# A transformer block's forward and backward on one core: the short fifth matmuls of dh in pairs of row halves, some transposes of the last head on TensorE with W_o's loads on ACT's queue, and W_q^T loaded at other places

## The chip, the core and the metric

The kernel runs on one core of a Trainium2 chip. A core has five engines with an instruction stream each: TensorE (PE, matrix multiplications into PSUM; its weight loads are listed as PEld), VectorE (DVE), ScalarE (ACT), GpSimd (POOL) and SyncE (SP), which here only issues DMA transfers. ACT and POOL issue transfers too. An engine works through its stream in order; semaphores make one engine wait for another, or for a transfer. The metric is the device time of one execution in microseconds (us); lower is better.

## The reference

The program takes one sequence of S = 2048 rows of D = 576 through a block with two branches, and returns the output and the gradients of the eight inputs (x, the K and V caches, and five weight matrices):

```python
def _A_ref(x, k_cache, v_cache, wq, wo):
    q = (x @ wq).reshape(B, Sq, H, Dh).transpose(0, 2, 1, 3)      # H 32, Dh 128
    scores = einsum("bhqd,bhkd->bhqk", q, k_cache) * (Dh ** -0.5)
    p = softmax(scores)
    o = einsum("bhqk,bhkd->bhqd", p, v_cache)
    return o.transpose(0, 2, 1, 3).reshape(B, Sq, H * Dh) @ wo

def _B_ref(x, w_gate, w_up, w_down):                              # F 4608
    g, u = einsum("bsd,df->bsf", x, w_gate), einsum("bsd,df->bsf", x, w_up)
    return einsum("bsf,fd->bsd", sigmoid(g) * u, w_down)

xn = layernorm(x)
out = x + _A_ref(xn, ...) * silu(_B_ref(xn, ...))
# and the vjp of out with grad_out, for x, k_cache, v_cache, wq, wo, w_gate, w_up, w_down
```

All matrices are bf16. Two gradients matter for what follows. With dO the gradient at the output of the second branch's last product, dh = dO @ w_down^T (2048 x 4608), du and dg are dh times two stored factors (`a_d` and `b_d`), and dw_up = xn^T @ du, dw_gate = xn^T @ dg, dw_down = h^T @ dO. The gradient at xn sums du @ w_up^T + dg @ w_gate^T + dq @ w_q^T.

## The kernel before, in words

Everything is tiled in P = 128 rows or columns; NT = 16 is the number of row tiles of S, DT = 5 the number of tiles of D. 576 is four tiles of 128 and one of KL = 64 columns; DL = 4 is the number of the short one. The stages run one after the other on TensorE:

- a1 (0 to 313 us): layernorm, gate and up projections. Full rows are multiplied at L295. The contraction over the 64 columns left over is done at L303 by pairs of matmuls on 64 of TensorE's 128 rows each, one for gate on the upper and one for up on the lower half. The stored factors a and b, and h, go to DRAM.
- a2 (to about 485): the product with w_down and what hangs on it.
- attention (to about 3655): 32 heads, one after the other but interlocked. Each head is laid on 64 positions of a programme written by hand: `at(pos, fn, ...)` enters a step at a position, `anchor` enters the steps that set the beat, and the list is then run in order of position. The order of the instructions on PE, DVE and ACT is that of the programme (`MAN`); SP's and POOL's streams are ordered by the tile framework's scheduler. A head makes P (the softmax numerators) and dS row tile by row tile, two tiles to a pair. Each pair is turned by a DMA transpose on SP (`trans_P`, `trans_dS`, issued at L603) into PT or dST, from four shared buffers (`wpt`), and PE's row products (L620, `acc<-Vn,PT` and `acc<-Kn,dST`) read these. L644 makes the column products from P and dS themselves. At the end of the last head five loads bring W_o, the heads' rows of it laid into two tiles no longer needed, by SP's queue (`load_wo`, L460).
- c1, the dO pass (to about 3807): for each row tile st, oT (the heads' outputs turned, by a DMA transpose on SP at L843, five buffers), times W_o at L872, 64 matmuls a tile; VectorE then forms the output row tile and doB = dO of the row tile, POOL loads three inputs two tiles ahead (`load_grp`, L849) and stores the output (L883). doB is turned into doBT by five TensorE transposes (L818) and two copies (`transpose_doB`). The fifth tile of doBT holds the 64 columns left over in its rows 64 to 127, and zeros above, which a memset puts there. w_down^T is loaded in three thirds of F columns (`wdT_h[0..2]`, L857, five transposes each on SP), the first third within this pass after row tiles 7, 8, 10, 11 and 12, and the others in b1.
- b1 (to about 4390): 18 blocks fb of 256 columns of F. In each: dh (L925, 16 row tiles x 5 matmuls into PSUM tiles of two row tiles; ACT copies each out at L929 as dhc, DVE multiplies it with the two factors at L930 and L931 to du_blk and dg_blk), dwd (`make_dwd`, L943, two halves, each of 16 row tiles times a 512-wide and a 64-wide matmul), the two products dwu and dwg (L967, accw, 64 matmuls each, in four groups of 16 row tiles), and their left-over 64 columns (L975, accl). The order of the engines' streams here is the scheduler's save for SP, whose order is written out.
- c2 (to about 4643): dw_q.
- c4 (to the end): the gradient at x, in eight blocks sbi of 256 rows, each in passes pi: three of du (cf), three of dg (cf), two of dq (cq) of 48 matmuls or more at L1101, into one set of PSUM accumulators a block. The first two blocks do their du and dg passes first, then their dq passes. Each pass starts with a DMA transpose on SP (L1088). W_q^T is loaded in four groups of eight heads, five DMA transposes each (`load_wqT`, `load_T_rows` at L92), after passes (0,3), (0,5), (1,1), (1,3) as (sbi, pi).

`turn` is a small job that later stages carry along: one DMA transpose of a stored gradient of K or V (L157), and the 512 KB store of the turn before (L160). There are 46 of them, spread over b1, c2 and c4; `turn(tkp, False)` only flushes the last store.

Of the kernel before, what the change touches and what calls it, by code (L numbers as in the profile page):

```python
# [95 lines left out]
def kernel(  # L96
# [80 lines left out]
    def kfull(i, kd):  # L177
        return P if KPAD else kd
# [243 lines left out]
    with tc.tile_pool(name="ld2", bufs=2) as ld2, tc.tile_pool(name="ld1q", bufs=1) as ld1q, \  # L422
# [19 lines left out]
        def at(pos, fn, *args):  # L442
            prog.append((pos, len(prog), fn, args))
# [13 lines left out]
        def load_wo(h0, h1):  # L457
            t_, o = (xnT, 0) if h0 < WX else (dsT, WX)
            dst = t_[:].rearrange("p i s -> p (i s)")[:, (h0 - o) * D:(h1 - o) * D].rearrange("p (h d) -> p h d", d=D)
            nc.sync.dma_start(dst, A_wo[h0 * P:h1 * P, :].rearrange("(h p) d -> p h d", p=P))  # L460

# [151 lines left out]
        class Box:  # L613
            pass

        def row_mm(bx, hs, T, rhs, qt, kt, sink):
            j = qt % GQ
            if j == 0 and kt == 0:
                bx.acc = ps_row.tile([P, GQ, P], f32, name="acc")
            nc.tensor.matmul(bx.acc[:, j, :], lhsT=T[qt][:, kt, :], rhs=getattr(hs, rhs)[:, kt, :],  # L620
                             start=(kt == 0), stop=(kt == NT - 1))
            if j == GQ - 1 and kt == NT - 1:
                sink(bx.acc)
# [185 lines left out]
    if True:  # L809
        pc2 = tc.alloc_tile_pool(name="pc2", bufs=1, reuse_waits="tile")  # L810
        doB = pc2.tile([P, NT, D], bf, name="doB")
        doBT = pc2.tile([P, DT, S], bf, name="doBT")
        nc.vector.memset(doBT[:P - KL, DL, :], 0.0)

        def transpose_doB(pool, st_):
            pt = pool.tile([P, 8, P], bf, name="pt", tag="tr")
            for j in range(DT):
                nc.tensor.transpose(pt[:, j, :], doB[:, st_, dlo[j]:dlo[j] + P], ident[:])  # L818
            cols = slice(st_ * P, (st_ + 1) * P)
            alt.copy(doBT[:, :DL, cols], pt[:, :DL, :])  # L820
# [8 lines left out]
        with tc.tile_pool(name="c1b", bufs=1, side="right", reuse_waits="tile") as blk, \  # L829
# [26 lines left out]
            def load_wdT(i, k=0):  # L856
                nc.sync.dma_start_transpose(wdT_h[k][:, i, :], B_w_down[k * FH:(k + 1) * FH, dlo[i]:dlo[i] + P])  # L857

            for st in range(NT):
# [30 lines left out]
        with tc.tile_pool(name="b1o", bufs=2, reuse_waits="tile") as outp, tc.tile_pool(name="b1k", bufs=2, reuse_waits="tile") as tkp, tc.tile_pool(name="b1t", bufs=3, reuse_waits="tile") as tmpp, \  # L890
                tc.tile_pool(name="b1r", bufs=2, reuse_waits="tile") as dblk, \
                tc.tile_pool(name="b1l", bufs=1, reuse_waits="tile") as ldp, \
                tc.tile_pool(name="b1ps", bufs=2, space=PSUM, reuse_waits="tile") as ps, \
                tc.tile_pool(name="b1pa", bufs=2, space=PSUM, reuse_waits="tile") as psa, \
                tc.tile_pool(name="b1pw", bufs=2, space=PSUM, reuse_waits="tile") as psw, \
# [16 lines left out]
            for fb in range(F // FB):  # L912
# [4 lines left out]
                dg_blk = dblk.tile([P, NT, FB], bf, name="dg_blk")  # L917
                def make_dh():
                    for st in range(NT):
                        srows = slice(st * P, (st + 1) * P)  # L920
                        if st % 2 == 0:
                            dh = ps.tile([P, 2, FB], f32, name="dh")
                        for i, (d0, kd) in enumerate(dts):
                            kk = kfull(i, kd)
                            nc.tensor.matmul(dh[:, st % 2, :], lhsT=doBT[:kk, i, srows], rhs=wdT_h[fb * FB // FH][:kk, i, fh], start=(i == 0), stop=(i == DT - 1))  # L925
                        if st % 2 == 1:
                            s2 = slice(st - 1, st + 1)
                            dhc = tmpp.tile([P, 2, FB], bf, name="dhc")
                            nc.scalar.copy(dhc[:], dh[:])  # L929
                            nc.vector.tensor_tensor(du_blk[:, s2, :], dhc[:], a_blk[:, s2, :], op=ALU.mult)  # L930
                            nc.vector.tensor_tensor(dg_blk[:, s2, :], dhc[:], b_blk[:, s2, :], op=ALU.mult)  # L931
                    nc.gpsimd.dma_start(du_d[:, fcols].rearrange("(t p) f -> p t f", p=P), du_blk[:])
                    nc.gpsimd.dma_start(dg_d[:, fcols].rearrange("(t p) f -> p t f", p=P), dg_blk[:])

# [15 lines left out]
                if fb == 0:  # L950
                    make_dwd(0)
                    make_dh()
                    make_dwd(1)
                else:
                    make_dh()
# [34 lines left out]
        with tc.tile_pool(name="c2b", bufs=1, reuse_waits="tile") as blk, tc.tile_pool(name="c2s", bufs=2, reuse_waits="tile") as sb, \  # L990
# [26 lines left out]
            for hg in range(NHG):  # L1017
# [43 lines left out]
        with tc.tile_pool(name="c4c", bufs=1, reuse_waits="tile") as chp, tc.tile_pool(name="c4s", bufs=2, reuse_waits="tile") as sb, \  # L1061
# [16 lines left out]
            NPF = 2 * (FT // FC)  # L1078
            accs_ = {}

            def do_pass(sbi, pi):
# [4 lines left out]
                scol = slice(sbi * SB2, (sbi + 1) * SB2)  # L1086
                ch = chp.tile([P, KC, SB2], bf, name=f"cq{pi % 2}" if nm == "cq" else f"cf{pi % 3}")
                nc.sync.dma_start_transpose(ch[:], src_d[scol, k0 * P:(k0 + KC) * P])  # L1088
# [83 lines left out]
```

## Time and profile before

| | us |
|---|---|
| median of three runs | 5063.81 |
| the three runs | 5054.67, 5063.81, 5084.64 |
| the profiled execution | 5069.4 |
| its span | 5067.4 |
| TensorE busy in it | 4914.0 |

The profile lists one execution. Times of rows are microseconds from the span's start. A group row of a view by line reads: line, engine, operation, what it writes and reads, tile size, shape and count, then busy time in us and mean ns of one, and after the last bar the idle time of the engine before it and what ended that. A row of a timeline reads: start, length, engine and line, with the idle time before it in brackets. A row of the waits reads: total us, times, the longest. The granted clock is the TensorE clock that the throttle allowed, as a share of full speed; ends of matmuls are modelled, so starts are the surer numbers. A DMA issue on a queue is shown as a row of that queue (SPq), and a row can gather several issues.

### The profile page before, as it was taken

The numbers are of one execution on the slowest core, as the hardware profiler recorded it, in microseconds if no ns is written. First come the engines' busy times: TensorE is split into PE (matmuls) and PEld (weight loads), VectorE is DVE, ScalarE is ACT, GpSimd is POOL, SyncE is SP. The second block draws the span as 40 slices with busy tenths as digits, with TensorE's granted clock in tenths as the row PEclk, the third lists the DMA queues.
The fourth block names the chain that finished last, engine by engine and source line by source line (L and its number), as shares of the span: only waits on it lengthen the run. The fifth ranks groups of instructions, "written<-read, shape, count | busy, mean of one in ns | idle before, by whom it ended". The sixth has DMA issues, their size and how long they took to land.

```text
span 5067.4 us, 107190 instructions
## 1 busy us (share of the span) xinstructions
PE 4914.0 (97%) x45178; PEld 3188.2 (63%) x45968; DVE 3098.3 (61%) x4853; ACT 2390.4 (47%) x3035; POOL 1504.2 (30%) x2197
## 2 busy tenths in 40 slices
PE   9998999999999999999999999999889999999999
PEld 3344777777766666666666666666547778755454
DVE  6555878887887888888788888888533222110101
ACT  5533656665666666566566666656302222100000
POOL 4322333333333333333333333332322323211000
PEclk9999999999999999999999999999999999999999
DMA  7875999999999999999999999999999988899996
GB/s 255 271 219 140 204 201 207 202 209 208 209 205 208 209 201 207 208 203 207 209 209 212 205 208 210 204 202 213 222 182 273 232 225 218 253 267 235 199 211 140
DMA packets 2865204, 1077.14 MB, mean 213 GB/s; under 512 B 2672336, under 2 KB 2795216, under 8 KB 2864720
## 3 DMA queue, kind: packets, MB, share of 16 engines
q1 hardware_dynamic: 2779456, 784.45, 86.6%
q0 software_dynamic: 85264, 285.79, 19.7%
q8 instruction: 359, 5.88, 0.5%
q14 instruction: 125, 1.02, 0.1%
HBM read 172.54 MB, written 225.12 MB: 78 GB/s over the span
## 4 chain that ended last, share of the span: by engine, by line
PE 84%; DVE 5%; issue 4%; DMA 3%; POOL 3%; SPq 0%; ACT 0%; DVEq 0%; POOLq 0%; ACTq 0%
PE acc L620 16%; PE acckv L644 9%; PE acc L1101 7%; PE sp L556 7%; PE dp L589 6%; PE accw L967 5%; PE acckv L641 5%; PE accp L513 4%; PE dh L925 3%; PE acc L392 3%; PE accd L943 3%; PE g_ps L295 2%; PE acc L1025 2%; PE u_ps L295 2%; PE acct L520 2%
## 5 line engine op out<-in xcount | busy, mean ns | idle before, releaser
L568 ACT ACTIVATE Pq<-sneg,nm 128x2048 bf16<-128x2048 bf16 x512 | 1025.9, 2004 | 212.0 <-DVE sneg L558 169.3
L592 DVE SCALAR_TENSOR_TENSOR dSq<-dp,delta,Pq 128x1024 bf16<-128x1024 f32 x608 | 770.8, 1281 | 390.8 <-PE dp L589 384.4
L620 PE MATMUL acc<-Kn,dST 128*128 128x128 bf16 x8192 | 955.2, 219 | 22.5 <-DMA dST<-dSq 6.4
L620 PE MATMUL acc<-Vn,PT 128*128 128x128 bf16 x8192 | 957.9, 219 | 15.9 <-DMA PT<-Pq 6.5
L620 PEld LDWEIGHTS <-dST 128*128 128x128 bf16 x8192 | 670.9, 98 | 363.9 <-DMA dST<-dSq 10.7
L620 PEld LDWEIGHTS <-PT 128*128 128x128 bf16 x8192 | 665.3, 98 | 329.8 <-DMA PT<-Pq 7.6
L558 DVE TENSOR_SCALAR_CACHE_REDUCE sneg<-sp,nm 128x1024 bf16<-128x1024 f32 x512 | 656.7, 1283 | 132.8 <-PE sp L556 101.1
L595 ACT ACTIVATE t<-dp,negdelta 128x1024 bf16<-128x1024 f32 x416 | 463.5, 1114 | 510.3 <-PE dp L589 419.8
L558 DVE TENSOR_SCALAR_CACHE_REDUCE sneg<-sp 128x1024 bf16<-128x1024 f32 x512 | 624.7, 1220 | 92.9 <-PE sp L556 45.7
L589 PE MATMUL dp<-VT,dOT 128*128 128x512 bf16 x1943 | 587.1, 379 | 26.4 <-DVE dSq L592 26.2
L556 PE MATMUL sp<-KT,QT 128*128 128x512 bf16 x1922 | 583.2, 380 | 7.3 <-DVE sneg L558 6.5
L644 PE MATMUL acckv<-Pq,dOn 128*128 128x512 bf16 x1312 | 487.5, 380 | 5.8 <-POOL dOn L576 5.8
L644 PE MATMUL acckv<-dSq,Qn 128*128 128x512 bf16 x1355 | 490.2, 380 | 1.2
L599 DVE TENSOR_TENSOR dSq<-t,Pq 128x1024 bf16<-128x1024 bf16 x416 | 304.5, 732 | 0.0
L576 POOL TENSOR_TENSOR dOn<-dOn,rinv_all 128x256 bf16<-128x256 bf16 x256 | 157.2, 614 | 390.2 <-DVE rinv_all L572 322.7
L967 PEld LDWEIGHTS <-xn_all 128*128 128x128 bf16 x2304 | 224.2, 98 | 27.8
L1117 DVE SCALAR_TENSOR_TENSOR junk<-dxn,xn_all 128x576 f32<-128x576 f32 x16 | 12.1, 758 | 370.9 <-ACT dxn L1112 370.9
L1101 PEld LDWEIGHTS <-cf 128*128 128x128 bf16 x2304 | 145.8, 98 | 145.6 <-DMA cf<-du_d 5.6
L513 PE MATMUL accp<-xnT,wq_h 128*128 128x512 bf16 x609 | 227.8, 384 | 4.4 <-ACT KT L40 1.1
L641 PE MATMUL acckv<-dOn,Pq 128*128 128x128 bf16 x2304 | 217.3, 219 | 2.8 <-POOL dOn L576 1.4
L674 POOL TENSOR_TENSOR prod<-ou,dOn 128x512 f32<-128x512 bf16 x128 | 154.8, 1209 | 207.5 <-ACT ou L40 206.7
L641 PE MATMUL acckv<-Qn,dSq 128*128 128x128 bf16 x2304 | 213.9, 219 | 1.4
(188 smaller groups left out, 7461.6 us busy)
## 6 DMA issues: line engine op xcount, KB each, us to landing
out_dram<-turn SPq DMA_DIRECT2D x46, 512.0 KB, 4.7
h_d<-h_row POOLq DMA_DIRECT2D x48, 384.0 KB, 2.9
a_d<-a_row POOLq DMA_DIRECT2D x48, 384.0 KB, 3.4
b_d<-b_row POOLq DMA_DIRECT2D x48, 384.0 KB, 4.5
a_blk<-a_d SPq DMA_DIRECT2D x18, 1024.0 KB, 6.0
b_blk<-b_d SPq DMA_DIRECT2D x18, 1024.0 KB, 21.7
du_d<-du_blk POOLq DMA_DIRECT2D x18, 1024.0 KB, 8.7
dg_d<-dg_blk POOLq DMA_DIRECT2D x18, 1024.0 KB, 11.7
```

Source lines behind the costliest of these rows:

```text
L513: nc.tensor.matmul(acc[:], lhsT=w[:, i, :], rhs=(srcT if i < DL else xnT)[:, i, cs], start=(i == 0), stop=(i == DL))
L556: nc.tensor.matmul(sp[:, c * CH:(c + 1) * CH], lhsT=hs.QT[:, qs], rhs=hs.KT[:, hf * HW_ + c * CH: hf * HW_ + (c + 1) * CH], start=True, st ...
L558: nc.vector.tensor_scalar(sneg[:, hf * HW_:(hf + 1) * HW_], sp[:], -SCALE, None if hf == 0 else nm[:, hf - 1:hf], op0=ALU.mult, op1=ALU.mi ...
L568: nc.scalar.activation(Pq, sneg[:], AF.Exp, bias=nm[:, hf:hf + 1], scale=-1.0, accum_out=hs.rs_all[:, qt:qt + 1])
L589: nc.tensor.matmul(dp[:, c * CH:(c + 1) * CH], lhsT=hs.dOT[:, qs], rhs=hs.VT[:, hf * HW_ + c * CH: hf * HW_ + (c + 1) * CH], start=True, s ...
L592: nc.vector.scalar_tensor_tensor(dSq[:, hsl], dp[:], hs.delta[:, qt:qt + 1], Pq[:, hsl], op0=ALU.subtract, op1=ALU.mult)
L595: nc.scalar.activation(t[:], dp[:], AF.Identity, bias=hs.negdelta[:, qt:qt + 1], scale=1.0)
L620: nc.tensor.matmul(bx.acc[:, j, :], lhsT=T[qt][:, kt, :], rhs=getattr(hs, rhs)[:, kt, :], start=(kt == 0), stop=(kt == NT - 1))
L641: nc.tensor.matmul(bx.acc[i][:, j * P:(j + 1) * P], lhsT=slabs[qt][:, k0 + j * P:k0 + (j + 1) * P], rhs=w, start=(qt == 0 and j == 0), sto ...
L644: nc.tensor.matmul(bx.acc[i][:], lhsT=w, rhs=slabs[qt][:, k0:k0 + CH], start=(qt == 0), stop=(qt == NT - 1))
L967: nc.tensor.matmul(acc[:kd, :FB], lhsT=xn_all[:, st, d0:d0 + kd], rhs=blk_[:, st, :], start=(st == 0), stop=(st == NT - 1))
L1101: nc.tensor.matmul(accs[sl][j][:, :nn], lhsT=ch[:, kk, sl * P:(sl + 1) * P], rhs=w_[:, n0:n0 + nn], start=(pi == 0 and kk == 0), stop=(las ...
```

## The change

The diff has five pieces.

1. dh in two halves. The 16 row tiles of a block are made as `make_dh(0)`, `make_dwd(0)`, `make_dh(1)`, `make_dwd(1)`. Each half first does the four full matmuls of its eight row tiles into four PSUM tiles, and then their fifth matmuls as four pairs: one of a pair on rows 0 to 63, the other, of a row tile two further on, on rows 64 to 127. For that both halves of the fifth tile of doBT and of wdT hold the same 64 columns: `transpose_doB` gets a third copy, `load_wdT` a DMA on POOL from the tile's lower to its upper half after the fifth transpose, and the memset goes. The PSUM pool of dh has four buffers in place of two, that of dwd one in place of two.
2. In the last head W_o is loaded in 15 pieces on ACT's queue, at positions 1.3 + 4k of the head, in place of five on SP's from position 50.
3. In the last head three pairs, P (14,15), dS (6,7) and dS (14,15), are turned on TensorE: 96 transposes into PSUM (`pe_pair`) with a copy out for each 8 or 16.
4. W_q^T's third and fourth groups are loaded after passes (1,3) and (1,5); the dq passes of the first two blocks alternate, (0,6), (1,6), (0,7), (1,7), and cq's buffers are counted through.
5. One turn less in c2 and one less in the second block of c4, so that as many places are left as there are turns, and the last flush stands behind the last block's stores.

```diff
-            nc.sync.dma_start(dst, A_wo[h0 * P:h1 * P, :].rearrange("(h p) d -> p h d", p=P))
+            nc.scalar.dma_start(dst, A_wo[h0 * P:h1 * P, :].rearrange("(h p) d -> p h d", p=P))
...
+        def pe_pair(T, pairs, qt, name, n, pool, tag, i, eng):
+            if i == 0:
+                t_ = wpt.tile([P, 2 * NT, P], bf, name=name, tag="PT")
+                for j in range(2):
+                    T[qt + j] = t_[:, j * NT:(j + 1) * NT, :]
+            pt = pool.tile([P, n, P], bf, name="ptr", tag=tag)
+            for m in range(n):
+                j, kt = divmod(i * n + m, NT)
+                nc.tensor.transpose(pt[:, m, :], pairs[qt][:, j, kt * P:(kt + 1) * P], ident[:])
+            j, kt = divmod(i * n, NT)
+            alt.copy(T[qt + j][:, kt:kt + n, :], pt[:], eng=eng)
...
-        WO_AT = 50.0
+        WO_AT = [(i, min(i + 2, 14)) for i in range(0, 14, 2)] + [(14, WX)] + [(i, min(i + 2, WX + WD)) for i in range(WX, WX + WD, 2)]
+        P_PE = {NT - 2: (35.5, 37.5, 39.5, 41.5)}
+        DS_PE = {6: (48.5, 50.5, 52.5, 54.5), NT - 2: (65.5, 67.0)}
...
-                    at(p1 + PT_AT, trans_P, hs, qt - 1)
-                    at(p2 + DST_AT, trans_dS, hs, qt - 1)
+                    if h == H - 1 and qt - 1 in P_PE:
+                        for i, p_ in enumerate(P_PE[qt - 1]):
+                            at(b + p_, pe_pair, hs.PT, hs.Pp, qt - 1, "PT", 8, ps_tr, "tr", i, "s")
+                    else:
+                        at(p1 + PT_AT, trans_P, hs, qt - 1)
...
-        for k, (h0, h1) in enumerate(((0, 8), (8, 16), (16, WX), (WX, WX + 7), (WX + 7, WX + WD))):
-            if h0 < H - 1:
-                at(bl + WO_AT + 3 * k, load_wo, h0, min(h1, H - 1))
+        for k, (h0, h1) in enumerate(WO_AT):
+            at(bl + 1.3 + 4 * k, load_wo, h0, h1)
...
-        nc.vector.memset(doBT[:P - KL, DL, :], 0.0)
...
             alt.copy(doBT[P - KL:, DL, cols], pt[P - KL:, DL, :])
+            alt.copy(doBT[:KL, DL, cols], pt[P - KL:, DL, :])
...
                 nc.sync.dma_start_transpose(wdT_h[k][:, i, :], B_w_down[k * FH:(k + 1) * FH, dlo[i]:dlo[i] + P])
+                if i == DL:
+                    nc.gpsimd.dma_start(wdT_h[k][:KL, DL, :], wdT_h[k][P - KL:, DL, :])
...
+                def make_dh(half):
+                    w_ = wdT_h[fb * FB // FH]
+                    sts = range(half * NT // 2, (half + 1) * NT // 2)
+                    dhs = [ps.tile([P, 2, FB], f32, name="dh") for _ in sts[::2]]
+                    for k, st in enumerate(sts):
+                        for i in range(DL):
+                            nc.tensor.matmul(dhs[k // 2][:, k % 2, :], lhsT=doBT[:, i, st * P:(st + 1) * P], rhs=w_[:, i, fh],
+                                             start=(i == 0 and k % 2 == 0), stop=False)
+                    for k in (0, 1, 4, 5):
+                        for j in range(2):
+                            rs = slice(j * KL, (j + 1) * KL)
+                            st = sts[k + 2 * j]
+                            nc.tensor.matmul(dhs[k // 2 + j][:, k % 2, :], lhsT=doBT[rs, DL, st * P:(st + 1) * P], rhs=w_[rs, DL, fh],
+                                             start=False, stop=(k % 2 == 1))
...
                 else:
-                    make_dh()
                     for fl in range(FB // P):
+                        make_dh(fl)
                         make_dwd(fl)
...
-                if hg < NHG - 1:
+                if hg < NHG - 2:
                     turn(tkp)
...
-                ch = chp.tile([P, KC, SB2], bf, name=f"cq{pi % 2}" if nm == "cq" else f"cf{pi % 3}")
+                ch = chp.tile([P, KC, SB2], bf, name=f"cq{next(ncq) % 2}" if nm == "cq" else f"cf{pi % 3}")
...
-                if sbi == 0 and pi in (3, 5):
-                    load_wqT((3, 5).index(pi))
-                elif sbi == 1 and pi in (1, 3):
-                    load_wqT(2 + (1, 3).index(pi))
-                elif sbi and sbi < NSB - 1 and (pi % 4 == 1 or (pi == 3 and sbi > 1)):
+                if (sbi, pi) in WQ_AT:
+                    load_wqT(WQ_AT.index((sbi, pi)))
+                elif 1 < sbi < NSB - 1 and pi in (1, 3, 5):
                     turn(tkp)
...
-            order_ = [(sbi, pi) for sbi in range(2) for pi in range(NPF)] + [(sbi, pi) for sbi in range(2) for pi in range(NPF, len(passes))]
+            order_ = [(sbi, pi) for sbi in range(2) for pi in range(NPF)] + [(sbi, pi) for pi in range(NPF, len(passes)) for sbi in range(2)]
```

More of the change, by code (lines that the diff above doesn't have):

```diff
@@ L1 @@
+import itertools
 from contextlib import ExitStack
@@ L782 @@
                 if qt % 2:
-                    at(p1 + PT_AT, trans_P, hs, qt - 1)
-                    at(p2 + DST_AT, trans_dS, hs, qt - 1)
+                    if h == H - 1 and qt - 1 in P_PE:
[3 more added lines that the diff above has]
+                        at(p1 + PT_AT, trans_P, hs, qt - 1)
+                    if h == H - 1 and qt - 1 in DS_PE:
+                        for i, p_ in enumerate(DS_PE[qt - 1]):
+                            if len(DS_PE[qt - 1]) == 4:
+                                at(b + p_, pe_pair, hs.dST, hs.dSp, qt - 1, "dST", 8, ps_tr, "tr", i, "s")
+                            else:
+                                at(b + p_, pe_pair, hs.dST, hs.dSp, qt - 1, "dST", NT, ps_big, "big", i, "sv"[i])
+                    else:
+                        at(p2 + DST_AT, trans_dS, hs, qt - 1)
                 if qt not in STT2:
@@ L917 @@
                 dg_blk = dblk.tile([P, NT, FB], bf, name="dg_blk")
[L918 to L933, printed above, removed]
@@ new lines, in make_dh @@
+                def make_dh(half):
[12 more added lines that the diff above has]
+                                             start=False, stop=(k % 2 == 1))
+                    for k, dh in enumerate(dhs):
+                        s2 = slice(sts[2 * k], sts[2 * k] + 2)
+                        dhc = tmpp.tile([P, 2, FB], bf, name="dhc")
+                        nc.scalar.copy(dhc[:], dh[:])
+                        nc.vector.tensor_tensor(du_blk[:, s2, :], dhc[:], a_blk[:, s2, :], op=ALU.mult)
+                        nc.vector.tensor_tensor(dg_blk[:, s2, :], dhc[:], b_blk[:, s2, :], op=ALU.mult)
+                    if half == 1:
+                        nc.gpsimd.dma_start(du_d[:, fcols].rearrange("(t p) f -> p t f", p=P), du_blk[:])
+                        nc.gpsimd.dma_start(dg_d[:, fcols].rearrange("(t p) f -> p t f", p=P), dg_blk[:])
@@ L1079 @@
             accs_ = {}
+            ncq = itertools.count()
+            WQ_AT = [(0, 3), (0, 5), (1, 3), (1, 5)]
             def do_pass(sbi, pi):
```

7 lines of the change are left out of this document (4 added, 3 removed).

## The prediction

> **What bounds the kernel now.** I read the page's head first, then the split of the span by stage, then what TensorE waited for in each stage the diff touches.
>
> ```profile
> span 5067.4 us, 107190 instructions
> PE 4914.0 (97%) x45178; PEld 3188.2 (63%) x45968; DVE 3098.3 (61%) x4853; ACT 2390.4 (47%) x3035; POOL 1504.2 (30%) x2197
> ...
> 3524.00:3653.00 129.00, 107.22 (x937) 68.53 (x953) 83.44 (x120) 59.80 (x65) 34.19 (x46) 0.93 1.14 220
> 3653.00:3807.00 154.00, 140.00 (x1158) 75.68 (x1177) 52.24 (x81) 8.37 (x33) 35.69 (x66) 0.97 1.15 193
> 3807.00:4390.00 583.00, 580.59 (x5402) 465.09 (x5441) 160.89 (x407) 128.55 (x261) 176.91 (x266) 1.00 0.90 237
> ```
>
> A stage row gives start and end, its length, then busy time of PE, weight load, DVE, ACT and POOL, the granted clock and the DMA share. TensorE bounds everything: 97% busy. So a change gains only by removing PE work or PE idle time. In the stage of dh (third row) PE is busy 580.59 of 583 us: there only matmul time counts. In the last head (first row) it idles 21.8 us at clock 0.93, in the dO pass (c1, second row) 14 us.
>
> **dh: what goes.** Per block of 256 columns, 16 fifth matmuls, padded with zeros to 128 rows, become 8 pairs of 64-row matmuls side by side.
>
> ```profile
> L925 PE MATMUL dh<-wdT,doBT 128*128 128x256 bf16 x1420 | 158.5, 273 | 0.2 <-ACT dhc L929 0.2
> L929 ACT CAST dhc<-dh 128x512 bf16<-128x512 f32 x144 | 84.2, 585 | 96.1 <-DVE du_blk L930 59.8 <-PE dh L925 33.3 <-DVE dg_blk L931 1.8
> L930 DVE TENSOR_TENSOR du_blk<-dhc,a_blk 128x512 bf16<-128x512 bf16 x144 | 61.1, 425 | 82.6 <-ACT dhc L929 77.1 <-DMA out_dram<-dwg 3.3 <-DMA a_blk<-a_d 2.2
> ...
> 3838.25 8.91 PE L925 MATMUL dh<-wdT,doBT 128*128 128x256 bf16 x80
> 3854.83 7.15 PE L967 MATMUL accw<-du_blk,xn_all 128*128 128x256 bf16 x64
> ...
> 3870.77 1.48 PE L925 MATMUL dh<-wdT,doBT 128*128 128x256 bf16 x12
> ```
>
> 80 matmuls start within 8.91 us; less the last one's own 0.273 that is 8.64/79 = 0.109 us each. Eight slots fewer: 8 x 0.109 = 0.87 us a block, 18 blocks: 15.7 us. But each half of dh now enters and leaves the 64-row mode once. Gate and up show that price:
>
> ```profile
> 198.86 0.81 PE L295 MATMUL u_ps<-wu_sb,xnT 128*128 128x512 bf16 x3
> 199.60 0.39 PE L303 MATMUL u_ps<-wl_sb,xnT 64*128 64x512 bf16 x1
> ...
> 203.92 0.38 PE L303 MATMUL g_ps<-wl_sb,xnT 64*128 64x512 bf16 x1
> 203.93 0.38 PE L303 MATMUL u_ps<-wl_sb,xnT 64*128 64x512 bf16 x1
> 204.23 0.60 PE L295 MATMUL g_ps<-wg_sb,xnT 128*128 128x512 bf16 x2
> ```
>
> A pair starts within 0.01 us (203.92, 203.93): pairs do overlap. Three full matmuls begin at 198.86, so at (0.81-0.38)/2 = 0.215 us apart the third begins at 199.29 and the pair 0.31 later: 0.10 lost going in. From 203.93 to 204.23 is 0.30: 0.09 lost coming out. So about 0.20 us an excursion, 0.41 for two, and 0.87-0.41 = 0.46 us a block; with 0.01 between pairs, 0.45 x 18 = 8.1 us. I take **-8.1**. Bounds: -15.7 if the switches cost nothing here, +8 if pairs did not overlap (the 0.41 and nothing saved).
> The page "TensorEngine Tiling (Array Packing)" of the Trainium skill, section Tiling Modes, says that changing the mode "drains the TensorE", which speaks against two excursions a block; the 0.10 us each way agrees. Its Overview's "Up to 2x" alone would make it -15.7.
>
> Cover of the rest: after the first half, products (one 0.585 cast, then eight DVE products of at most 0.425: 4.0 us) run under the first dwd, which takes half of the time of both (from 80 x 0.109 us after the start of dh to 3854.83: 7.9 us), 3.9 us, and what dh's second half needs of it, the first of four PSUM tiles, is free after one cast; after the second half under the second dwd and the 15 accw matmuls (1.6 us) that come ahead of the one that reads the last product: 5.5 us of cover for 4.0. dwd's single PSUM tile is copied during the next half of dh (4 us). The third doBT copy goes on ACT or DVE, busy 8 and 52 of 154 us in the dO pass. If the cover were gone, each us past it costs 18.
>
> **The last head.** PE's waits there, the chain of waits, and SP's queue:
>
> ```profile
> PE acc L872 <- DMA oT<-on_d: 7.4, 1, 7.4
> PE acc L620 <- DMA PT<-Pq: 6.1, 3, 4.5
> PE acc L620 <- DMA dST<-dSq: 3.6, 2, 2.9
> ...
> 3626.76 9.48 DMA dST<-dSq
> 3638.40 8.97 DMA oT<-on_d
> ...
> 3546.86 0.58 SPq L460 DMA_DIRECT2D xnT<-in_A_wo_dram  x1
> ...
> 3596.86 41.25 SPq L603 DMA_TRANSPOSE dST<-dSq  x7
> ...
> 3587.38:3594.21 6.83, 5.63 (x31) 3.75 (x33) 1.88 (x2) 1.70 (x2) 1.16 (x2) 0.50 1.13 230
> 3641.99:3652.23 10.24, 4.60 (x27) 3.17 (x29) 0.00 (x0) 0.00 (x0) 1.56 (x3) 0.50 1.11 263
> ```
>
> The queue on SP runs without a gap (7 transposes in 41.25 us, 5.9 each): transposes are late because the queue is full. The three wait rows sum to 17.1 us. Each of the two long ones is followed by a stretch at half clock (last two rows), at granted clock 0.50, in which 5.63 and 4.60 us of busy time would have been half, 2.8 and 2.3. So 22 us hang on the late transposes.
> The change takes three transposes (3 x 5.9 = 17.7 us) and five W_o loads (0.58 each) off SP, so SP reaches oT about 18 us earlier by its own count, or when its input is there. TensorE takes 96 transposes in their place: I price them by these.
>
> ```profile
> L520 PE MATMUL acct<-ident,Vn x504: 216/219/219, 489.6 to 3541.2; 128*128 128x128 bf16 x168
> L40 ACT COPY VT<-acct 128x1024 bf16<-128x1024 bf16 x2 | 2.0, 1002 | 2.2 <-PE acct L520 2.2
> ```
>
> Eight in a row take about 8 x 0.055 us (half the 256-column slot of 0.109), so 96 cost 5.3 us of PE; eight ACT copies at 1.0 us, and one of twice that width on ACT and on DVE each, fit in the 69 us in which ACT does nothing. W_o's 15 issues on ACT at 0.58 us are 8.7 us more, between its copies; queued behind them are the exps that feed the products, so some of it may show (0 to 3 us).
> The wait on PT goes with its half clock, -6.1-2.8, and that on dST, -3.6. The seventh dST (12,13), behind which oT is issued, now starts at 3596.86 + 6 x 5.9 = 3632.3; two of the three transposes taken off lie ahead of it on SP with little else to wait for, so oT itself would issue at 3632.3 + 5.9 - 2 x 5.9 = 3626.4 and land 9.0 us later, 3635.4. PE reached it at 3647.4 - 7.4 = 3640.0 and comes 7.2 us earlier (-12.5 for the waits, +5.3): 3632.8. So 2.6 of the 7.4 stay, the half clock behind it (2.3) goes: -7.1. In all -6.1-2.8-3.6-7.1+5.3 and 1.3 for ACT's issues: **-13.0**. Bounds: 0 (the transposes stay as late, and the added work hides in the waits) and -20.
> "DMA: Bandwidth & Descriptors" of the Trainium skill, section Issuing engines are not separate DMA queues, says that DMAs issued by different engines run on the same 16 DMA engines and interleave, so moving W_o to ACT saves only issue time. The DMA share of 1.14 in this stage agrees that they are full; by that rule the W_o part is worth nothing, and the whole gain comes from the three transposes.
>
> **The dO pass (c1).** Two things are queued on POOL:
>
> ```profile
> PE acc L872 <- DMA oT<-on_d: 12.3, 2, 9.8
> ...
> 3771.50 0.54 POOL L849 DMA_DIRECT2D dsb<-dsil_d  x1
> ...
> 3742.23 35.12 DMA oT<-on_d x2
> 3789.19 3.36 SPq L857 DMA_TRANSPOSE wdT<-in_B_w_down_dram  x2
> ```
>
> The 12.3 us of oT stalls are a transfer stream as full as before (35.12 us for two), and PE's pace gives its buffers back, so they stay. New: POOL's copy of wdT's half waits for the fifth wdT transpose, the last on SP (3789.19 + 3.36), and the loads for the last two row blocks (now issued by 3771.50) and the stores queue behind it; DVE waits for these, PE for DVE. With SP some 14 us earlier the copy is released at about 3779. In step with PE, 13 us earlier, these loads would issue by 3758.5, so they are 20 us later in PE's terms; one row block takes PE 154/16 = 9.6 us, and they are issued about two blocks ahead of use, 19 us, so little of it shows. I put +2, bounds 0 and +10. With the last head that is **-11**.
>
> **W_q^T and the last passes.**
>
> ```profile
> 4681.32 7.73 SPq L92 DMA_TRANSPOSE wqT<-in_A_wq_dram  x5
> 4695.28 6.05 PE L1101 MATMUL acc<-wuT_sb,cf 128*128 128x512 bf16 x47 [3.12 <-DMA cf<-du_d]
> 4696.17 6.67 SPq L92 DMA_TRANSPOSE wqT<-in_A_wq_dram  x5
> 4709.20 3.37 PE L1101 MATMUL acc<-wgT_sb,cf 128*128 128x512 bf16 x17 [1.99 <-DMA cf<-dg_d]
> 4710.04 1.71 SPq L157 DMA_TRANSPOSE turn<-dkT_d  x1
> 4711.80 31.42 SPq L1088 DMA_TRANSPOSE cq<-dq_d  x4
> 4710.36:4713.77 3.41, 3.41 (x15) 1.44 (x14) 0.00 (x0) 0.00 (x0) 0.00 (x0) 0.50 1.08 222
> ```
>
> The third and fourth groups (7.73, 6.67 us of SP) move two passes later, past the loads that were late: 3.12 + 1.99 go, and half of the 3.41 us at half clock: 6.8. But SP has the same groups and loads ahead of the first cq as now, less the turn (1.71): it issues at 4710.1 and lands 31.42/4 = 7.9 us on, 4718.0. PE, two passes of 5.9 us (48 of the matmuls of which 47 took 6.05) after 4709.2 - 3.1 - 2.0, wants it at 4715.9: about +2.1, with what the delay of the groups themselves adds 2.4. **-4.4**, bounds -7 and -1.
>
> **The tail.** One turn fewer in the passes leaves the last turn's store for the end.
>
> ```profile
> 5060.38 4.25 SPq L1130 DMA_DIRECT2D out_dram<-dx  x2
> out_dram<-turn SPq DMA_DIRECT2D x46, 512.0 KB, 4.7
> ```
>
> Now the last dx is issued by 5064.63 and the span ends 2.8 us later. The 512 KB store is issued behind it, and takes 4.7 us, so it lands at 5069.3, and with the 0.7 us that it is quicker without other traffic (my guess) at 5068.6. dx landed at about 5066 (the span ends 1.4 us after): **+2.6** (bounds +2, +4).
>
> **Sum.** -8.1 - 11 - 4.4 + 2.6 = -20.9 us. The profiled execution took 5069.4 us (2.0 of it outside its span): 5048.5. The median of the three runs is 5063.81, 0.11% less, so I predict 5048.5 x 5063.81/5069.4 = **5043**, -0.41%. What a measurement here can tell from no change is about 0.5%, 25.3 us: my forecast lies inside.
>
> **The rivals** (all against the median).
> 1. *More goes than I credit.* Switches cost less between 256-column matmuls (dh near -13), the last head gains -18, and the stream that starts 18 us earlier carries through the dO pass, so that 5 of its 12.3 us go: -13-18-5-5+2.6 = -38, 5026. For it: SP's queue is full from the last head to 3792. Against: PE sets when oT buffers come free.
> 2. *The last head gives it back.* W_o interleaves with the transposes as before, ACT's issues delay the exps, oT waits for PE-made dST all the same: 0 there, -8.1-4.4+2.6 = -10, 5054. For it: DMA share 1.14. Against: 17.7 us less to transpose.
> 3. *Slower: accw waits for the products.* One place: the first accw of each block. The products of the second half queue on DVE and ACT behind dwd's and dw's copies; each block then waits x us more. It decides from x = (8.1+12.8)/18 = 1.2 us; at 1.5 us: 1.5 x 18 - 20.9 = +6, 5070. Against: 5.5 us of cover for 4.0, ACT and DVE busy under 30% there.
> 4. *dh's pairs don't pair*, but run one after the other: +8 for -8.1, so -5, 5059. Against: overlapping pairs in the rows above.
>
> **Numbers.** Chances: forecast 0.50 (5035 to 5051), rival 1 0.22, rival 2 0.15, rival 3 0.08, rival 4 0.05. The likeliest is 5043. The range 5016 to 5072 takes in rivals 1, 2 and 4, all the better bounds but the last, and rival 3 at 1.5 us. Faster by over 0.5% (under 5038.5): rival 1 and 0.36 of the forecast's share, 0.40. Within: 0.52. Slower by over 0.5%: that rival 3 at 2.7 us a block or more, or something unseen: 0.08.
>
> **What would show it.** dh: the start of one block to the next, 32.52 us now (3870.77 - 3838.25), should be 32.07; 31.65 says switching is free, 32.9 says no overlap, and accw waiting on du_blk or dg_blk says rival 3. Last head: no PE wait on PT, oT's down to about 2 us, the end of attention 13 us earlier; rival 2 if oT still takes 7. dO pass: POOL waiting for wdT, DVE for g2b, xb or dsb. c4: one cf wait left of three, one on cq instead. Tail: the last landing is out_dram<-turn. I am wrong if the block period rises, or if attention ends no earlier.

## The result, and the profile after

The changed kernel takes 5039.85 us (median of 9 runs, 5026.62 to 5060.83) against 5063.81 us (median of 9, 5049.17 to 5084.64): ratio 0.995, 95% interval 0.9932 to 0.9968. The forecast was 5043 in a range of 5016 to 5072. Run again later (e5, below) the ratio was 0.9971 (0.996 to 0.9983); the two together speak for about 0.4%. The profiled execution of the changed kernel took 5040.4 us, its span 28.8 us less than before.

Its head and its stages, as before (start and end, length, busy time of PE, weight load, DVE, ACT and POOL, granted clock, DMA share):

```profile
span 5038.6 us, 108246 instructions
PE 4950.9 (98%) x46064; PEld 3173.8 (63%) x46064; DVE 3086.9 (61%) x4861; ACT 2398.0 (48%) x3052; POOL 1508.5 (30%) x2200
...
3526.00:3651.75 125.75, 118.11 (x1113) 77.19 (x1111) 85.10 (x122) 68.96 (x74) 36.07 (x50) 0.97 1.13 212
3651.75:3780.90 129.15, 129.15 (x1097) 68.60 (x1096) 45.87 (x81) 13.16 (x37) 34.24 (x63) 1.00 1.13 209
3780.90:4359.90 579.00, 578.21 (x5481) 447.91 (x5478) 154.19 (x412) 121.08 (x266) 178.72 (x269) 1.00 0.92 241
4613.70:5039.00 425.30, 410.09 (x3331) 210.38 (x3328) 50.34 (x128) 14.67 (x65) 17.25 (x32) 0.99 0.90 185
```

The second stage row is the surprise: the dO pass had 14 us of idle PE and half clock before, and has none now, 129.15 us busy of 129.15.

To place the 28.8 us I cut both traces at the same instructions: the first exp of the last head, the fourth matmul on oT (before it stand three that run ahead of the rest), the first dh, the last accl, the first pass of the last stage, its last matmul, the end. Both kernels were profiled twice (e5 and e6 are the same kernels once more). Lengths in us:

```
                               before   after   before, e6   after, e5
start to last head             3528.4   3530.4     3523.2      3543.9
last head to oT (4th matmul)    131.9    121.4      127.7       121.3
dO pass to first dh             144.0    129.2      142.9       129.2
dh to last accl                 587.0    578.9      587.0       578.9
to the last passes              251.7    253.9      252.1       252.5
the last passes                 417.1    416.7      414.5       413.9
tail                              7.3      8.2        7.3         8.2
span                           5067.4   5038.6     5054.7      5047.9
```

The first row is unchanged work, and moves by 20 us from one execution to another: this is a large part of the runs' scatter. From the last head on the change saves 30.8 us in the first pair of profiles and 27.5 in the second; the parts below are read there, because whole times cannot tell them.

dh first. Two blocks' rows of the changed kernel's timeline:

```profile
3814.54 3.67 PE L951 MATMUL dh<-wdT,doBT 128*128 128x256 bf16 x32
3818.14 0.61 PE L957 MATMUL dh<-wdT,doBT 64*128 64x256 bf16 x8
3818.68 4.09 PE L977 MATMUL accd<-doB,h_blk 128*128 128x512 bf16 x32
3822.61 3.66 PE L951 MATMUL dh<-wdT,doBT 128*128 128x256 bf16 x32
...
3846.61 3.67 PE L951 MATMUL dh<-wdT,doBT 128*128 128x256 bf16 x32
```

From 3814.54 to 3846.61 the block period is 32.07 us, to the hundredth the forecast. Eight row-half matmuls (four pairs) and the way back take from 3818.14 to 3818.68, 0.54 us; four plain slots of 0.109 would be 0.44, so 0.10 is lost coming out; going in, the last full one of the 32 started at 3814.54 + 3.67 - 0.273 = 3817.94, 0.20 ahead of the first pair, another 0.09. No PE wait on du_blk or dg_blk stands in the stage.

PE's waits from shortly before the last head to oT, and in the last passes; and POOL's queue in the dO pass (between them two stretches at half clock, as stage rows):

```profile
PE acc L899 <- DMA oT<-on_d: 4.2, 1, 4.2
PE dp L590 <- DVE dSq L593: 1.5, 2, 0.8
PE acc L633 <- DVE dq_n L704: 1.4, 2, 0.9
...
PE acc L1137 <- DMA cq<-dq_d: 4.1, 2, 3.9
PE acc L1137 <- DMA cf<-du_d: 2.5, 1, 2.5
PE accq L1080 <- DVE dwq L43: 1.2, 1, 1.2
...
3637.33:3644.15 6.82, 5.65 (x33) 3.73 (x34) 0.00 (x0) 0.00 (x0) 0.54 (x2) 0.50 1.10 257
4692.04:4695.46 3.42, 3.42 (x17) 1.44 (x16) 0.00 (x0) 0.00 (x0) 0.00 (x0) 0.50 0.90 201
...
3765.01 0.54 POOL L884 DMA_DIRECT2D wdT<-wdT  x1 [13.90 <-PE pt L842]
3765.54 0.57 POOL L874 DMA_DIRECT2D g2b<-g_d  x1
```

The waits on PT and dST are gone; oT's is 4.2 us for 7.4. In the last passes one wait on cf is left, but that on cq has 3.9 us. Behind oT's wait and behind cq's the clock was 0.50 for a while. POOL is indeed blocked for 13.9 us (the row names PE, but what comes last is the fifth wdT transpose, which landed at 3764.28), and the last tiles' loads go out at 3765 and after; the PE wait that could follow, pt on DVE's doB, is 0.5 us, for 0.7 before. And the tail:

```profile
5030.70 4.25 SPq L1166 DMA_DIRECT2D out_dram<-dx  x2
5034.99 0.43 SPq L161 DMA_DIRECT2D out_dram<-turn  x1
```

The 512 KB store is the last transfer; it landed at 5037.72, 1.3 us behind dx.

### The profile page after: what moved, and what is told of

It is laid out like the page before. It is cut to its first block, busy times and chain, and to the rows that moved or that the text cites. A ratio compares the mean times of both kernels' runs of the same rounds, so it can differ in the third digit from the quotient of the medians.

```text
span 5038.6 us, 108246 instructions
## 1 busy us (share of the span) xinstructions
PE 4950.9 (98%) x46064; PEld 3173.8 (63%) x46064; DVE 3086.9 (61%) x4861; ACT 2398.0 (48%) x3052; POOL 1508.5 (30%) x2200
## 4 chain that ended last, share of the span: by engine, by line
PE 86%; issue 4%; DVE 4%; POOL 3%; DMA 2%; SPq 1%; ACT 0%; DVEq 0%; POOLq 0%; ACTq 0%
PE acc L633 15%; PE acckv L657 11%; PE sp L557 8%; PE acc L1137 7%; PE dp L590 7%; PE accw L1002 5%; PE acckv L654 4%; PE accp L514 4%; PE accd L977 3%; PE acc L393 3%; PE g_ps L296 3%; PE acc L899 3%; PE dh L951 2%; PE u_ps L296 2%; PE acc L1060 2%
## 5 line engine op out<-in xcount | busy, mean ns | idle before, releaser
L590 PE MATMUL dp<-VT,dOT 128*128 128x512 bf16 x2048 | 609.5, 379 | 25.9 <-DVE dSq L593 25.8
L557 PE MATMUL sp<-KT,QT 128*128 128x512 bf16 x2048 | 610.8, 380 | 6.7 <-DVE sneg L559 6.5
L657 PE MATMUL acckv<-Pq,dOn 128*128 128x512 bf16 x1472 | 544.8, 379 | 5.9 <-POOL dOn L577 5.9
L657 PE MATMUL acckv<-dSq,Qn 128*128 128x512 bf16 x1472 | 534.9, 380 | 0.0
L514 PE MATMUL accp<-xnT,wq_h 128*128 128x512 bf16 x640 | 239.4, 384 | 2.7 <-ACT KT L41 1.1
## 6 DMA issues: line engine op xcount, KB each, us to landing
dg_d<-dg_blk POOLq DMA_DIRECT2D x18, 1024.0 KB, 11.8
```

Source lines behind the costliest of these rows:

```text
L514: nc.tensor.matmul(acc[:], lhsT=w[:, i, :], rhs=(srcT if i < DL else xnT)[:, i, cs], start=(i == 0), stop=(i == DL))
L557: nc.tensor.matmul(sp[:, c * CH:(c + 1) * CH], lhsT=hs.QT[:, qs], rhs=hs.KT[:, hf * HW_ + c * CH: hf * HW_ + (c + 1) * CH], start=True, st ...
L590: nc.tensor.matmul(dp[:, c * CH:(c + 1) * CH], lhsT=hs.dOT[:, qs], rhs=hs.VT[:, hf * HW_ + c * CH: hf * HW_ + (c + 1) * CH], start=True, s ...
L657: nc.tensor.matmul(bx.acc[i][:], lhsT=w, rhs=slabs[qt][:, k0:k0 + CH], start=(qt == 0), stop=(qt == NT - 1))
```

## The experiments

**e1: the dh part alone**, in the kernel before (halves, pairs, third doBT copy, wdT's POOL copy; nothing else of the diff).

> The kernel before with the dh part alone (halves, row-half pairs, third doBT copy, the POOL copy of wdT's half). Theory (pairs save 0.87 us a block, two mode excursions take back 0.41): b1 from the first dh to the last accl 587.0 -> 579.0 us, block period 32.07 us, no PE wait on du_blk or dg_blk; ratio 0.998 to 0.999. Rival A (the halves' order or the copies cost): period above 32.3. About c1 in this trace: if the 14.8 us that c1 lost between the two profiles come from SP reaching oT earlier, c1 here keeps some 12 us of PE waits on oT, as before; if those waits are an accident of one execution's transfers, they are anywhere from 0 to 15 us.

5051.68 us, ratio 0.9988 (0.9972 to 1.0004). The block period, from one block's accl to the next, was 32.07 us in all 17 intervals. The stage took 583.9 us, 4.9 more than the changed kernel's, all of it in the first block. PE's and DVE's waits there:

```profile
PE dh L926 <- ACT dhc L937: 3.4, 2, 3.2
...
DVE dg_blk L939 <- DMA b_blk<-b_d: 3.4, 1, 3.4
```

b_blk of the first block landed 14.2 us after its issue, DVE's products stood, and the four PSUM tiles of dh came free late; 3.4 us at half clock followed. The halves have this weak spot in the first block, where the factors' loads are late; in the changed kernel's profile PE waited 0.3 us there. The dO pass took 140.9 us with oT waits, as before.

**e2: four excursions a block in place of two.** In the changed kernel the pairs are done after each four row tiles:

```diff
                     for k, st in enumerate(sts):
+                        if k == 4:
+                            pairs_(0)
                         for i in range(DL):
...
-                    for k in (0, 1, 4, 5):
+                    pairs_(4)      # the same two pair slots for k in (q, q + 1)
```

> The changed kernel with four excursions into the 64-row mode a block in place of two (two pair slots after each four row tiles). Theory (0.20 us an excursion): block period 32.07 + 0.41 = 32.48 us, b1 +7.4 us. Rival (switches cost little and the missing half of the gain sits elsewhere, in the second-half order): period within 0.1 of the changed kernel's.

5047.61 us, ratio 0.9973 (0.9953 to 0.9992). A block in its timeline:

```profile
3812.06 1.80 PE L960 MATMUL dh<-wdT,doBT 128*128 128x256 bf16 x15
3813.79 0.39 PE L954 MATMUL dh<-wdT,doBT 64*128 64x256 bf16 x4
3814.11 1.92 PE L960 MATMUL dh<-wdT,doBT 128*128 128x256 bf16 x16
3815.97 0.39 PE L954 MATMUL dh<-wdT,doBT 64*128 64x256 bf16 x4
...
3846.28 0.39 PE L954 MATMUL dh<-wdT,doBT 64*128 64x256 bf16 x4
```

From 3813.79 to 3846.28 is a period of 32.49 us, 0.42 over the changed kernel's: 0.21 us an excursion, and the stage 6.9 us longer. So the price of a mode change, read from gate and up in another stage at another width, holds here.

**e3: the last head's part alone**, in the kernel before.

> The kernel before with the last head's changes alone (W_o on ACT's queue, three pairs turned by TensorE). Theory 1 (the earlier SP stream carries through c1): last head -10 us and c1's oT waits gone as in the changed kernel, first dh some 24 us earlier after the same start of attention; ratio about 0.995. Theory 2 (c1's waits are an accident of the execution): last head -10 us, c1's PE waits on oT anywhere from 0 to 15 us, whichever head stands ahead of it.

5051.68 us, ratio 0.9989 (0.9976 to 1.0001). Last head 121.1 us. But the dO pass took 137.4 us, with PE waits on oT in it:

```profile
PE acc L896 <- DMA oT<-on_d: 5.0, 2, 4.2
```

So the earlier stream does not by itself clear the dO pass: against theory 1, which I had formed from one pair of profiles.

**e4: W_q^T's groups, the dq passes' order and the turns alone.**

> The kernel before with the W_q^T groups, the dq passes' order and the turns alone. Theory (as the changed kernel's trace has it): the first two blocks of the last stage keep about 8 us of PE idle and half clock, now 4 us of it in front of the first dq pass, so the stage gains under 1 us, and the end loses 1 us to the last turn's store; ratio 0.999 to 1.001. Rival (my forecast): -4.4 us in the stage. c1 here, with the head of before, again tells whether its oT waits of 12 us repeat.

5055.43 us, ratio 1.000 (0.9986 to 1.0013). PE's waits from the start of its last passes:

```profile
PE acc L1103 <- DMA cq<-dq_d: 2.1, 1, 2.1
PE acc L1103 <- DMA cf<-du_d: 0.8, 1, 0.8
```

The last passes took 412.8 us. Taking all profiles, this stage took 410.8 to 417.5 us in the six with this part, mean 414.7, and 414.0 to 418.7 in the eight without it, mean 415.8: about 1 us, inside the spread. The tail, 8.7 us, lost 1.3. With the head of before the dO pass here took 136.5 us, not 144.

**e5 and e6: both kernels unaltered, once more.**

> The changed kernel unaltered, once more. Theory 1 (the stream that starts earlier on SP carries c1 through): c1 from the second oT matmul group to the first dh 129 us again, no oT wait but the first. Theory 2 (slow stretches of transfers fall into c1 in any kernel, for 30 to 90 us, and how long is an accident): c1 anywhere from 129 to 138 us, with the rate of small transfer packets in the slow stretch at about half of attention's. Both: block period 32.07, last head 121 us, ratio 0.994 to 0.997.

> The kernel before unaltered, once more. Theory 1: c1 141 to 144 us with some 12 us of oT waits. Theory 2: anywhere from 130 to 144. Both: last head 131 us, block period 32.52.

e5 5048.96 us, ratio 0.9971 (0.996 to 0.9983); e6 one run, 5056.67 us. The dO pass took 129.2 and 142.9 us again (the table above).

**e7 and e8: the two halves of the last head's part**, each in the kernel before: the three pairs turned by TensorE with W_o still on SP, and W_o on ACT's queue with all pairs turned by DMA.

> The kernel before with the three pairs turned by TensorE, W_o's five loads still on SP's queue. Theory (the queue of transposes is what is late, W_o's issues take 0.6 us each of it and their bytes the same engines wherever they are issued): last head 121 to 124 us, the PT wait gone, nearly the whole of the 10 us. Rival (W_o's place matters, its 5 MB among the transposes hold them up): 126 us or more, with a wait on PT or dST left.

> The kernel before with W_o in 15 loads on ACT's queue alone, all transposes by DMA. Theory: last head 128 to 132 us, waits on PT, dST and oT nearly as before (6.1, 3.6, 7.4 us). Rival: 126 us or less, since the loads come early in the head and leave the late transposes alone.

e7 5053.65 us, ratio 0.9985 (0.9968 to 1.0002), last head 123.0 us; e8 5064.83 us, ratio 0.9998 (0.9985 to 1.0011), last head 134.9 us. PE's waits of e7 and of e8:

```profile
PE acc L632 <- DMA PT<-Pq: 2.9, 1, 2.9
PE acc L897 <- DMA oT<-on_d: 2.2, 1, 2.2
```

```profile
PE acc L871 <- DMA oT<-on_d: 8.2, 1, 8.2
PE acc L620 <- DMA dST<-dSq: 6.4, 2, 4.1
PE acc L620 <- DMA PT<-Pq: 3.3, 2, 2.9
```

TensorE's turning of three pairs is nearly the whole gain of the last head; W_o's place alone moves the waits about (17.9 us in sum, 17.1 before) and saves nothing. With the pairs off SP it may be worth some 1.7 us: the PT wait that e7 keeps is gone in e3 and in the changed kernel, and their last heads took 121.1 and 121.4 us. The section Issuing engines are not separate DMA queues of "DMA: Bandwidth & Descriptors" in the Trainium skill has the transfers of all issuing engines on the same 16 DMA engines, so that another issuer saves only time of issue; for W_o, e8 agrees, with its ratio of 0.9998.

The dO pass took 129.2 us in e8, whose pairs all go through SP as before, and 129.2 in e7. So the stalls don't go with one kernel or the other. What the profiles with stalls have in common is a stretch of slow transfers: oT's slowest landing in the whole pass was 20.1 to 25.3 us in ten of the eleven profiles with POOL's loads of g2b, xb and dsb (e9 included), and 14.6 in e8. Where the stretch lasts, POOL's loads are late as well. DMA traffic of the changed kernel in its slow stretch, 3668 to 3698 us (queue, packets, MB, share of 16 engines; then issues, KB each, median us to landing):

```profile
DMA packets 9372, 4.35 MB, mean 145 GB/s; under 512 B 8913, under 2 KB 8913, under 8 KB 9370
q1 hardware_dynamic: 8683, 2.21, 83.1%
q0 software_dynamic: 687, 2.11, 37.9%
g2b<-g_d POOLq DMA_DIRECT2D x4, 144.0 KB, 11.9
oT<-on_d SPq DMA_TRANSPOSE x4, 19.0
```

The engines are busy, but moved 145 GB/s where the stage row of the last head has 212. That led to the last runs, on POOL's software-built transfers (q0).

**e10: the kernel before without the group loads.** `load_grp` loads for the first two row tiles only, and these are used for all others.

> The kernel before with the loads of g2b, xb and dsb in the dO pass left out after the second row tile (the first two are used again, so the first output, dO and what follows from it are computed from the wrong rows). Theory (POOL's loads, 0.44 MB a row tile beside the transposes, make the slow stretch): small transfer packets stay at 550 to 800 per us through the pass, c1 129 us. Rival (the stretch comes from the transposes' own reads or from elsewhere): rates of 250 to 450 per us for 30 us or more, as in the kernels with the loads.

One run, 5057.71 us. No slow stretch: oT's slowest landing 10.2 us, dO pass 129.2 us, with the head of before.

**e9: oT's first matmul behind attention's, and an earlier last store**, in the changed kernel:

```diff
+                        if st == 0 and h == 0 and j == 0:
+                            tc.keep_in_program_order(mm)
...
+                elif sbi == NSB - 1 and pi == 1:
+                    turn(tkp, False)
```

> The changed kernel with two small edits: the first matmul of the dO pass is kept behind all of attention's matmuls on TensorE (three of oT's matmuls stand some 190 instructions ahead of their place in the changed kernel, and PE waits 4.2 to 4.9 us there for oT), and the last turn's store goes out in the last block's second pass. Theory: no PE wait on oT before the dO pass, no half clock behind it, last head to first dh 5 to 8 us shorter than the changed kernel's 250.5 where c1 has no slow stretch, tail 7.3 us instead of 8.2; ratio to before about 0.994. Rival: PE then waits for the last dST copies or for oT's second tile instead, and under 2 us is gained.

5041.48 us, ratio 0.9966 (0.9946 to 0.9986). PE's waits in the last head:

```profile
PE acc L633 <- DVE dq_n L704: 1.8, 3, 0.9
PE acc L633 <- DMA PT<-Pq: 1.2, 2, 0.8
PE acckv L657 <- POOL dOn L577: 0.8, 1, 0.8
```

The wait on oT is gone there, last head 116.6 us, 4.7 less than the changed kernel's, tail 6.9. This profile's dO pass met a slow stretch, waited 2.8 us on oT and took 133.8, 4.6 more than without stalls, so that what the last head gave was spent. The ratio can't be told from that of the changed kernel.

**e11 and e12: the group loads on ACT's queue**, in e9's kernel and in the kernel before:

```diff
-                        nc.gpsimd.dma_start(t_[:], src[st_ * P:(st_ + 1) * P, :])
+                        nc.scalar.dma_start(t_[:], src[st_ * P:(st_ + 1) * P, :])
```

> The kernel of e9 with the dO pass's loads of g2b, xb and dsb issued on ACT's queue in place of POOL's. Theory (the slow stretch of the transposes comes from POOL's software-built transfers beside them, since without the loads there was none): no stretch of 30 us or more under 450 packets per us in the dO pass, c1 129 us, last head 116 to 117 us, ratio 0.993 to 0.996. Rival (any such traffic beside the transposes, from whichever queue, makes the stretch, or it is an accident): stretches of 30 to 90 us as in eight of the nine profiles with the loads up to e8 and in e9.

> The kernel before with the same loads on ACT's queue alone. Theory: no slow stretch, c1 129 us in place of 143 to 144, ratio about 0.997 to 0.999. Rival: stretch and waits on oT as in the two profiles of before, c1 over 136 us, ratio 1.000.

e11 5043.57 us, ratio 0.9955 (0.9937 to 0.9973); e12 5064.00 us, ratio 0.9994 (0.9973 to 1.0016). In both profiles the dO pass took 129.2 us and oT's slowest landing was 14.0 and 12.0 us. The same 30 us of e12's traffic, with the group loads now on q10:

```profile
DMA packets 20131, 7.24 MB, mean 241 GB/s; under 512 B 18209, under 2 KB 20001, under 8 KB 20129
q1 hardware_dynamic: 17921, 4.55, 90.3%
q10 hardware_dynamic: 2016, 2.07, 21.9%
g2b<-g_d ACTq DMA_DIRECT2D x4, 144.0 KB, 4.5
oT<-on_d SPq DMA_TRANSPOSE x5, 10.9
```

The loads are as many bytes as before, and the transposes' queue moves 4.55 MB where it moved 2.21. In the slowest 30 us of its dO pass this queue moved 2.1 to 3.2 MB in ten of the eleven profiles with POOL's loads and 4.2 in e8; with the loads on ACT's queue it moved 4.3 in e11 and 4.1 in e12, and without the loads 3.6 in e10, when it kept the engines busy only 56.2% of the time. So three profiles without POOL's loads have no slow stretch, and ten of eleven with them have one (nine of the ten before e9, where the expectation of e11 counts eight of nine). What it is about POOL's loads stays open: on ACT's queue they were also issued at other times (in e12 those of the second row tile 12.5 us earlier against the pass, those from the fifth on 1 to 2 us earlier), and no run separates the two. In the times no gain can be told: the five profiles with the pairs turned by SP and with POOL's loads lost 9.5 us in the pass on average (14.8, 11.8, 7.4, 13.7 and none in e8), which would be a ratio of 0.998, and e12's interval holds that as well as no gain. e11 is the shortest of all from the last head on (1499.7 us in the profile; the changed kernel 1508.2 and 1504.0, before 1539.0 and 1531.5), but by its time it is no better than the changed kernel.

## Why the prediction came out right, step by step

- **dh, -8.1 us:** shown. 8.0 us in the stage, period 32.07. The eight slots, the 0.2 us an excursion and the cover of the products each held; e1 has the same period without the rest, and e2 prices the excursion at 0.21. One cost was not in the forecast: the row to the last passes took 252.5 to 253.9 us in the six profiles with the dh part and 251.7 to 252.1 in the eight without, about 1.3 us more on average. PE waits there on the tile onb, 0.3 to 1.5 us, in each of the six and in none of the eight; why it comes later there was not tested.
- **Last head, -13.0 us:** measured -10.5 against the first profile of before and -6.4 against the second. The working holds in its parts. The 96 transposes took 5.36 us of PE (forecast 5.3). Set back by the 2.0 us by which the last head started later, oT issued at 3627.1 (forecast 3626.4), PE reached it at 3632.3 (3632.8), and the data at 3636.4 (3635.4). Its wait shrank by 3.2 instead of 4.8, and the half clock behind it did not go, which I had counted at 2.3: of the 6.82 us at 0.50 that stand behind the new wait 5.65 are busy, 2.8 us of loss. And the waits to be removed are not the same in each execution: 17.1 us in the profile that I read, 12.2 in e6 (4.5 on dST, 4.3 on oT, 3.4 on PT).
- **dO pass, +2 us:** wrong, by 16.8 us in the profiled pair. The step that failed is "so they stay": I took oT's stalls for a fixed property of a stream as full as before. The row itself spoke against that: 35.12 us for two transposes of oT, where one had taken 8.97 at the end of attention. The traces show stalls where a slow stretch meets a stream with little lead (how long before the pass's own first matmul the second oT is issued). SP's queue before, and after:

```profile
3638.40 5.00 SPq L843 DMA_TRANSPOSE oT<-on_d  x1
3643.51 5.42 SPq L603 DMA_TRANSPOSE dST<-dSq  x1
3648.98 18.47 SPq L843 DMA_TRANSPOSE oT<-on_d  x3
...
3629.13 40.13 SPq L868 DMA_TRANSPOSE oT<-on_d  x6
```

Before, the second oT was issued at 3648.98, 11.3 us ahead of the pass's own work, and now at 3634.33, 17.4 us ahead, since no dST stands between the first two. All ten profiles with a slow stretch can be set side by side. With a lead of 11.3 to 11.5 us the pass lost 14.8, 11.8, 7.4 and 13.7 us (before, e1, e4, e6) and 4.6 in e9. With a lead of 15.7 to 17.4 it lost nothing in four (after, e2, e5, e7) and 8.2 us in e3. Without a slow stretch it lost nothing at a lead of 10.8 to 11.1 (e8, e10, e11, e12). In e9 PE no longer waits for oT ahead of the pass and reaches it earlier, so that the lead is 11.4 again, and 4.6 of the 4.7 us saved in the last head are lost in the pass. So the lead covers most of these stretches; e3 shows that it need not, and no run changes the lead and nothing else. The +2 for POOL's blocked queue was nothing: the wait is there, 13.9 us long, and DVE had the slack.

- **W_q^T, -4.4 us:** measured -0.5 and -0.7 in the two pairs. The two cf waits went as worked out. What was mis-sized, in the first pair: the new waits on cq, 4.1 us for 2.4; the half clock of 3.42 us behind them, 1.7 more, which I had not priced though the long waits of the last head each had one behind them; and the cf wait that stays, 2.5 for 1.8. That is 4.1 us, the whole difference within 0.2. In the second pair cq's waits were 2.6 us, near the forecast, but there the kernel before had 6.1 us of cf waits with no half clock behind them, and the changed one has the half clock. By all profiles the part is worth about 1 us.
- **Tail, +2.6 us:** +0.9. The store landed 2.7 us after issue, not 4: with only the last store of dx beside it, it is quicker than the 4.7 us of the median row.
- **Sum:** -20.9 forecast; -30.8 and -27.5 in the profiles from the last head on; -24.0 and -14.8 by the medians. The forecast lies between the last two, and in that it was lucky: the gain that I denied the dO pass made up for what W_q^T and the last head fell short. Rival 1 named that gain (the stream carries through the dO pass), with 5 us of it and at 0.22; its price was two thirds too low in this pair of profiles. Rivals 3 and 4 fell with the period; rival 2 fell with the last head, though its premise, that W_o's place alone is worth nothing, is what e8 shows. By whole times the three parts alone (0.9988, 0.9989 and 1.000) add up to 0.23%, less than the whole's 0.50 and 0.29; their intervals leave that open. One chance was put wrongly: the 0.08 for slower by over 0.5% takes in all of rival 3, whose own price of 5070 is within 0.5%.

## What to carry to other kernels

A price read from one stage of a trace (a mode change) carried over to another stage within 0.01 us; a stall read from one trace was there again in other executions of the same code, but in another size (17.1 and 12.2 us of waits in the last head; 14.8, 13.7 and, in e4, 7.4 us lost in the dO pass). Before forecasting that a DMA stall stays or goes, look whether the transfer behind it is slow by its own work or by a stretch in which everything in flight is late, and how far ahead of its use it is issued. And where a wait on a transfer is replaced by a shorter one, price the half clock behind it again: it stood behind nearly every PE wait of over 3 us in these profiles, save the one at the very start.

## What the runs showed of the hardware

Beside POOL's loads the transposes of the dO pass had a slow stretch in ten of eleven profiles: landings of 20 to 25 us, and 2.21 MB moved in 30 us of the changed kernel's. With the same bytes loaded over ACT's queue they had none in two profiles: 4.55 MB in the same 30 us of e12, and landings of 14.0 us at most in the pass. The section of the Trainium skill named above has the transfers of all issuing engines on the same 16 DMA engines, with only time of issue to be saved by another issuer; by that section alone the queue would make no difference to the transposes, and in these profiles it went with one. Why, and whether it is so in runs without a profile, stays open.
